# A spectral layer and two MLPs on one core: batch 0's stores moved between batch 1's loads, the inverse 64-point transform on unsplit float32, the front without GpSimd, and the last transform woven into the stages beside it

## Chip, cores and metric

The kernel runs on one core of a Trainium2 chip. The metric is the device time of one execution in microseconds, the median of several runs. Lower is better.

## What is computed

Two batches of 3008 tokens with 256 channels go through a Fourier layer along the tokens, and the 6016 resulting rows through two MLPs with 2048 hidden units. Inputs of the Fourier layer are float32, the MLP weights float64.

```python
X = np.fft.rfft(x, axis=1)                      # x: [2, 3008, 256]
Yr = Xr @ w_r - Xi @ w_i + b_r                  # Xr, Xi: parts of X
Yi = Xr @ w_i + Xi @ w_r + b_i
Y = soft_threshold(Yr, 0.01) + 1j * soft_threshold(Yi, 0.01)
h = np.fft.irfft(Y, n=3008, axis=1).reshape(6016, 256)
h = h @ w_in1;  h = np.maximum(h, 0) + alpha * np.minimum(h, 0)
h = (h @ w_out1) @ w_in2
out = np.where(h >= 1, h, np.where(h <= -1, 0, (h + 1) ** 2 / 4)) @ w_out2
```

## The kernel before

3008 is 47 x 64, so both transforms are made in two radices with matrices as TensorE's operands. The work stands in one written order for each engine; the framework adds the waits.

*Phase 1* (line 254, tiles `ps`, `ae`): 16 groups, 8 for each batch. A group loads 4 rows of `x`, TensorE makes the length-47 transform, ScalarE evicts one half (L256) and VectorE the other (L258) into `ae`, and SP's queue stores it to DRAM (`a_dr`) in two halves of 48 partitions (`store_a(g, 0)` and `store_a(g, 1)`, L223). Batch 0's stores stand after all sixteen loads.

*Phase 2* (L287 to L374): 24 items, 12 for each batch. `f2` (L295) makes the length-64 transform of an item from `a` (read back from `a_dr` by `load_a`, L219) and a third of the matrices in `m_t[i // 4]` (the thirds are called m0 to m2, each good for four items; `n32` holds the inverse ones, n0 to n2). ScalarE copies the result rounded to 12 bits (`fh`, L300) and once more negated (L301); VectorE makes the rest (`fl`, L302) and its negation (L303). `mix` is the complex channel mixing: 24 matmuls, three for each product, with high and low parts. VectorE adds the bias and applies the soft threshold (L320 to L322). `split_y` splits the result into `yh` (ScalarE) and `yl` (GpSimd, L330), and `i1` makes the inverse length-64 transform of it in three matmuls for each of two products. ScalarE evicts into `ve` (L341), two items to a buffer and two buffers in turn (`c2`, `c3`), and SP stores each full buffer to `v_dr`. The matrices for `i1` are split too, into `n_h` (`split_n`). One pass of the loop over j, a step, runs `f2` of item j+2, `mix` of item j and `i1` of item j-2.

*Phase 3*: `p3` reads `v_dr` back as `v` in 16 groups and makes the inverse length-47 transform (L404), transposed, into `y`; each group has two halves c, one evicted by ScalarE (L408) and one by VectorE (L410).

*MLPs* (L413 to L498): 2 layers x 12 chunks of 512 tokens (the sixth of each batch has 448) x 16 blocks f of 128 hidden units. `prep` splits a chunk of `y` into `mxh` and `mxl`, in blocks `c0`, `c1` or `c2`, `c3` in turn (`c0` and `c1` hold the mixing weights `wm` before). `first` makes six matmuls into `psh`; two activations (L431, L432) and a VectorE operation (L433) make the first layer's nonlinearity, whose result is split into `gh` and `gl`; `second`, three blocks behind, adds six matmuls into `pso`.

*Weights*: `conversions` is a generator that turns the float64 weights of block f into a high and a low float32 part (`wt`). A block takes loads into `u` (ScalarE's queue, L127 and L129), three activations (L139, L140, L155), four VectorE operations (L141, L167, L152, L157) and three GpSimd ones (L158, L160, L161). A call of `next(conv)` does half of one block and half of the block beside it; block f of a layer must be ready before `first` of f in chunk 0. Layer 0 has 35 calls.

PSUM has two sets of four buffers, `h` (of `f2`, `first`, one half of `p3`) and `o` (of `mix`, `i1`, `second`, the other half).

Of the kernel before, what the change touches and what calls it, by code (L numbers as in the profile page):

```python
# [75 lines left out]
def spectral_mlp_kernel(ctx: ExitStack, tc: tile.TileContext, x, w_r, w_i, bias, c_f1, c_f2,  # L76
# [152 lines left out]
    for g in range(8):  # L229
        load_x(g)  # L230
    m_t = [block(f"m{k}", [128, 8, 128], F32, f"m{k}") for k in range(3)]
    nc.sync.dma_start(m_t[0][:, 0:4, :].rearrange("p k f -> p (k f)"), c_f2[:, 0:512])
    wm32 = [rot.tile([128, 2, D], F32, tag="tb", name=f"wm32_{k}") for k in range(2)]
    nc.sync.dma_start(wm32[0], w_r.rearrange("(c p) e -> p c e", p=128))
    nc.sync.dma_start(wm32[1], w_i.rearrange("(c p) e -> p c e", p=128))
    nalpha = base.tile([128, NF], F32, name="nalpha")
    nc.sync.dma_start(nalpha, alpha)
    g47 = base.tile([96, 128], F32, name="g47")
    nc.sync.dma_start(g47, c_i2)
    for g in range(8, 16):  # L240
        load_x(g)
    for g in range(16):
# [17 lines left out]
        if g > 7:  # L260
            store_a(g, 1)
        if g == 7:
            load_a(0, A_PARTS[:2])
            nc.sync.dma_start(m_t[0][:, 4:8, :].rearrange("p k f -> p (k f)"), c_f2[:, 512:1024])
            load_a(0, A_PARTS[2:3])
            for k in range(8):
                store_a(k, 1)
            n32 = [block(f"w{k}", [128, 8, 128], F32, f"n32_{k}") for k in range(3)]
            b_t = base.tile([128, 1, D], F32, name="b_t")
            nc.sync.dma_start(b_t[:, 0, :], bias)  # L270
            load_mn(0, n32, c_i1)
            load_mn(1, m_t, c_f2)
            load_a(0, A_PARTS[3:])
            load_mn(1, n32, c_i1)
            load_mn(2, m_t, c_f2)
            load_mn(2, n32, c_i1)
# [4 lines left out]
    n_h = []  # L281

    def split_n(g):
        n_h.append(block(f"m{3 + g}", [128, 2, 4, 128], F32R, f"n{g}"))
        split(n32[g // 2][:, 4 * (g % 2):4 * (g % 2) + 4, :], n_h[g][:, 0], n_h[g][:, 1], A)

# [59 lines left out]
    vs = {}  # L346

    def load_v(g):
        b, j = divmod(g, 8)
        vs[g] = piece([96, 4, D], F32, f"v{b}_{j}")  # L350
        nc.sync.dma_start(vs[g], v_dr[b][:, 4 * j:4 * j + 4, :])

    conv = conversions(0, list(range(NF)), 0)
    n = len(items)
    for j in range(2):
        f2(*items[j])
    for j in range(n):
        if j + 2 < n:
            f2(*items[j + 2])
        if j >= 1:  # L360
            split_y(*items[j - 1])
        mix(*items[j])
        if j + 2 >= n:
            for g in range(2):
                load_v(2 * (j + 2 - n) + g)
        if 5 <= j < 10:
            load_a(1, A_PARTS[j - 5:j - 4])
        if j % 2 == 0 and j < 12:
            split_n(j // 2)
        if j >= 2:  # L370
            i1(*items[j - 2])
        if 4 <= j < 22:
            next(conv, None)
    split_y(*items[n - 1])  # L374

# [19 lines left out]
    y = [block(f"a{b}", [128, 2, S], F32, f"yt{b}") for b in range(B)]  # L395

    def p3(g):
        b, j = divmod(g, 8)
        while len(vs) < min(g + NP, 16):
            load_v(len(vs))  # L400
        ps = [psum.tile([128, 4, 128], F32, tag="ho"[c], name=f"ps3_{b}_{j}_{c}") for c in range(2)]
        for c in range(2):
            for i in range(4):
                T.matmul(ps[c][:, i, :], vs[g][:, i, c * 128:(c + 1) * 128], g47, start=True, stop=True)  # L404
        for c in range(2):
            dst = y[b][:, c, 376 * j:376 * j + 376].rearrange("p (i n) -> p i n", i=4)
            if c == 0:
# [121 lines left out]
```

## Time and profile before

| | |
|---|---|
| runs | 1253.16 us median of 3 (1252.68 to 1253.88) |
| profiled execution | span of 1251.2 us from its first to its last instruction; what lies around the span makes the rest of a run's time |
| TensorE | busy 1214.9 us (97%), weight loads 1030.1 (82%) |
| VectorE | busy 964.8 us (77%) |
| ScalarE | busy 584.6 us (47%) |
| GpSimd | busy 186.2 us (15%) |
| DMA | 59.32 MB, a mean of 47 GB/s |

The shares are means over stages that differ much: in the first hundred microseconds the DMA engines are nearly full, and from about 250 us on they hardly work. PE is TensorE, PEld its weight loads, DVE is VectorE, ACT ScalarE, POOL GpSimd and SP the engine that only issues transfers. ACTq and SPq are the issuing sides of ScalarE and SP.

### The profile page before, as it was taken

To read this page: it belongs to the slowest core of one execution; us is meant where nothing else is said; L and a number is where in the kernel's file an instruction comes from. 1 tells how busy PE (TensorE), PEld (TensorE's weight loads), DVE (VectorE), ACT (ScalarE), POOL (GpSimd) and SP (SyncE) were. 2 spreads that over 40 slices of the span, in tenths; PEclk is the share of its full clock that TensorE was granted. 3 is DMA by queue.
4 is the path that set the end of the run, shared out by engine and by line. 5 is a ranking of instruction groups with operands and counts; after the bars stand their busy time and mean duration, and the time that the engine had idled before them with its cause. 6 is when DMAs were issued, how large, how long until landed. Compare 5 with 4: busy or idle time off the path is not lost.

```text
span 1251.2 us, 15881 instructions
## 1 busy us (share of the span) xinstructions
PE 1214.9 (97%) x5910; PEld 1030.1 (82%) x5910; DVE 964.8 (77%) x1455; ACT 584.6 (47%) x1073; POOL 186.2 (15%) x136
## 2 busy tenths in 40 slices
PE   8898889899999999999999999999999999999998
PEld 6798888688888898888888978888888888888887
DVE  2589977978988899877777798777776777677765
ACT  2355545445455555444444554444444444444443
POOL 0136664401313131300000131000000000000000
PEclk9899999999999999999999999999999999999999
DMA  9983284010000100000000200000000000000000
GB/s 259 304 278 108 87 236 134 1 51 18 30 21 18 34 18 17 1 1 1 1 1 1 65 3 13 5 17 18 1 18 18 15 1 17 17 3 15 17 18 16
DMA packets 37182, 59.32 MB, mean 47 GB/s; under 512 B 3248, under 2 KB 25200, under 8 KB 37104
## 3 DMA queue, kind: packets, MB, share of 16 engines
q1 hardware_dynamic: 23536, 41.37, 10.6%
q10 hardware_dynamic: 13568, 16.93, 4.2%
q8 instruction: 46, 0.75, 0.3%
q14 instruction: 32, 0.26, 0.1%
HBM read 39.55 MB, written 18.74 MB: 47 GB/s over the span
## 4 chain that ended last, share of the span: by engine, by line
PE 83%; DVE 5%; POOL 4%; issue 4%; DMA 2%; ACT 1%; SPq 0%; ACTq 0%; POOLq 0%; DVEq 0%
PE pso L96 13%; PE pso L95 13%; PE pso L97 13%; PE psh L96 13%; PE psh L95 13%; PE psh L97 13%; PE ps L404 2%; POOL yl L330 2%; DMA x<-in_x 1%; DVE gl L92 1%; DVE ta L433 1%; PE ps L254 1%; DVE gh L91 1%; POOL cm L160 1%; PE psf L295 1%
## 5 line engine op out<-in xcount | busy, mean ns | idle before, releaser
L96 PE MATMUL pso<-gl,w 128*128 128x512 f32 (+1 forms) x768 | 298.8, 389 | 6.2 <-DVE gl L92 6.2
L95 PE MATMUL pso<-gh,w 128*128 128x512 f32 (+1 forms) x768 | 297.1, 387 | 3.9 <-DVE gh L91 3.9
L96 PE MATMUL psh<-mxl,w 128*128 128x512 f32 (+1 forms) x768 | 297.2, 387 | 0.0
L95 PE MATMUL psh<-mxh,w 128*128 128x512 f32 (+1 forms) x768 | 296.9, 387 | 0.0
L97 PE MATMUL pso<-gh,w 128*128 128x512 f32 (+1 forms) x768 | 296.3, 386 | 0.0
L97 PE MATMUL psh<-mxh,w 128*128 128x512 f32 (+1 forms) x768 | 295.9, 385 | 0.0
L92 DVE TENSOR_TENSOR gl<-ta,gh 128x512 fp32r<-128x512 f32 (+1 forms) x384 | 280.1, 729 | 7.2 <-ACT gh L89 0.6
L437 ACT ACTIVATE ta<-psh 128x512 f32<-128x512 f32 (+1 forms) x192 | 113.1, 589 | 281.3 <-PE psh L97 247.1
L438 DVE SCALAR_TENSOR_TENSOR tb<-ta 128x512 f32<-128x512 f32 (+1 forms) x192 | 131.2, 683 | 137.5 <-ACT ta L437 136.5
L431 ACT ACTIVATE ta<-psh 128x512 f32<-128x512 f32 (+1 forms) x192 | 113.1, 589 | 250.8 <-PE psh L97 211.8
L433 DVE SCALAR_TENSOR_TENSOR ta<-ta,nalpha,tb 128x512 f32<-128x512 f32 (+1 forms) x192 | 168.9, 880 | 64.3 <-ACT tb L432 63.7
L96 PEld LDWEIGHTS pso<-gl,w 128*128 128x128 f32 x768 | 144.5, 188 | 36.9 <-DVE gl L92 10.5
L95 PEld LDWEIGHTS pso<-gh,w 128*128 128x128 f32 x768 | 144.3, 188 | 33.4 <-DVE gh L91 5.3
L95 PEld LDWEIGHTS psh<-mxh,w 128*128 128x128 f32 x768 | 144.5, 188 | 28.4
L97 PEld LDWEIGHTS psh<-mxh,w 128*128 128x128 f32 x768 | 144.3, 188 | 27.7
L97 PEld LDWEIGHTS pso<-gh,w 128*128 128x128 f32 x768 | 144.5, 188 | 27.3
L96 PEld LDWEIGHTS psh<-mxl,w 128*128 128x128 f32 x768 | 144.4, 188 | 27.0
L440 DVE TENSOR_TENSOR ta<-psh,tb 128x512 f32<-128x512 f32 (+1 forms) x192 | 129.2, 673 | 0.0
L89 ACT ACTIVATE gh<-ta 128x512 fp32r<-128x512 f32 (+1 forms) x192 | 118.3, 616 | 2.0 <-DVE ta L440 2.0
L158 POOL TENSOR_TENSOR cp<-cp,u 128x512 f32<-128x512 f32 x32 | 44.7, 1397 | 462.4 <-DVE cp L157 454.0
L432 ACT ACTIVATE tb<-psh 128x512 f32<-128x512 f32 (+1 forms) x192 | 112.4, 585 | 0.0
L91 DVE CAST gh<-ta 128x512 fp32r<-128x512 f32 (+1 forms) x192 | 91.1, 474 | 19.5
(62 smaller groups left out, 1067.3 us busy)
## 6 DMA issues: line engine op xcount, KB each, us to landing
u<-in_w_in ACTq DMA_DIRECT2D x32, 256.0 KB, 2.8
u<-in_w_out ACTq DMA_DIRECT2D x32, 256.0 KB, 3.0
v_dr<-ve SPq DMA_DIRECT2D x12, 512.0 KB, 3.3
v<-v_dr SPq DMA_DIRECT2D x16, 384.0 KB, 7.1
x<-in_x SPq DMA_DIRECT2D x15, 384.0 KB, 8.8
out<-yt SPq DMA_DIRECT2D x20, 256.0 KB, 2.2
a<-a_dr SPq DMA_DIRECT2D x6, 768.0 KB, 7.9
a_dr<-ae SPq DMA_DIRECT2D x20, 192.0 KB, 7.9
```

The costliest lines, as they stand in the source:

```text
L89: A.activation(hi, src, AF.Copy)
L91: V.tensor_copy(hi, src)
L92: V.tensor_tensor(lo, src, hi.bitcast(F32), op=ALU.subtract)
L95: T.matmul(ps, wl, xh, start=start, stop=False)
L96: T.matmul(ps, wh, xl, start=False, stop=False)
L97: T.matmul(ps, wh, xh, start=False, stop=stop)
L431: A.activation(ta, ps, AF.Relu, scale=-1.0)
L432: A.activation(tb, ps, AF.Relu)
L433: V.scalar_tensor_tensor(ta, ta, nalpha[:, f:f + 1], tb, op0=ALU.mult, op1=ALU.add)
L437: A.activation(ta, ps, AF.Relu, bias=0.5, scale=0.5)
L438: V.scalar_tensor_tensor(tb, ta, 1.0, ta, op0=ALU.min, op1=ALU.mult)
L440: V.tensor_tensor(ta, ps, tb, op=ALU.max)
```

## The change

- Phase 1: `store_a(g, 0)` of batch 0 stands right after its group, between the loads of batch 1; the second halves follow all loads. Batch 1's groups store their first halves together and then their second halves. `load_a(1)` follows these in one piece, with nalpha and g47 ahead of it.
- `i1` takes float32 operands as they are, one matmul for each product in place of three; `split_y`, `split_n` and their tiles go. The matrices are called `n_t`.
- The negation L303 is ScalarE's.
- Layer 0's conversions run wholly on VectorE and ScalarE; layer 1's on GpSimd as before, started at chunk 2 instead of chunk 1.
- `p3` of batch 0 stands in steps 16 to 23 of phase 2, one group a step; that of batch 1 in the first MLP, one half with each block from block 4 of chunk 0 to block 3 of chunk 1, evicted by ScalarE. `v` has buffers of its own.
- In chunk 0 the split of the activation is one block late and its high part is ScalarE's.
- `prep(0, 0)` stands in step 22.

```diff
-    def convert_w(l, f, part, clamp=None):
+    def convert_w(l, f, part, clamp, low_engine):
+        E = low_engine
...
-            G.tensor_tensor(p, p, low, op=ALU.mult)
+            E.tensor_tensor(p, p, low, op=ALU.mult)
...
-            G.tensor_tensor(m, m, wt[l, f][:, 0, :].bitcast(F32), op=ALU.subtract)
-            G.tensor_tensor(wt[l, f][:, 1, :], m, p, op=ALU.add)
+            E.tensor_tensor(m, m, wt[l, f][:, 0, :].bitcast(F32), op=ALU.subtract)
+            E.tensor_tensor(wt[l, f][:, 1, :], m, p, op=ALU.add)
...
+    for g in range(8):
+        f1(g)
         store_a(g, 0)
...
+        load_x(8 + g)
+        if g == 3:
+            nc.sync.dma_start(m_t[0][:, 0:4, :].rearrange("p k f -> p (k f)"), c_f2[:, 0:512])
...
+    load_a(0, A_PARTS[:3])
+    nc.sync.dma_start(m_t[0][:, 4:8, :].rearrange("p k f -> p (k f)"), c_f2[:, 512:1024])
+    nc.sync.dma_start(b_t[:, 0, :], bias)
+    load_mn(0, n_t, c_i1)
+    for g in range(8):
+        store_a(g, 1)
+    load_mn(1, m_t, c_f2)
+    load_a(0, A_PARTS[3:])
+    for g in range(8, 16):
+        f1(g)
+        store_a(g, 0)
+    load_mn(1, n_t, c_i1)
+    for g in range(8, 16):
+        store_a(g, 1)
+    load_mn(2, m_t, c_f2)
+    load_mn(2, n_t, c_i1)
+    nc.sync.dma_start(nalpha, alpha)
+    nc.sync.dma_start(g47, c_i2)
+    load_a(1, A_PARTS)
...
-        V.tensor_scalar(xl[:, :, 0:64], xl[:, :, 128:192].bitcast(F32), -1.0, None, op0=ALU.mult)
+        A.mul(xl[:, :, 0:64], xl[:, :, 128:192].bitcast(F32), -1.0)
...
-            q, r = divmod(2 * i + k, 4)
-            mm3(ps[:, k, :], n_h[q][:, 0, r, :], n_h[q][:, 1, r, :], yh[:, k, :], yl[:, k, :], True, True)
+            T.matmul(ps[:, k, :], n_t[i // 4][:, (2 * i + k) % 8, :], y32[:, k, :], start=True, stop=True)
...
+    def late_split(step):
+        return step[0] == 1 or step[:2] == (0, 0)
+
     def split_late(step):
-        if step is not None and step[0] == 1:
+        if step is not None and late_split(step):
...
+    conv = conversions(0, list(range(NF)), V, V)
...
+        if j == 13:
+            for g in range(3):
+                load_v(g)
+        if j >= P3_AT:
+            g = j - P3_AT
+            p3(g, 0, A)
+            p3(g, 1, V)
+            if g + 3 < 8:
+                load_v(g + 3)
+        if j == n - 2:
+            prep(0, 0)
+        for _ in range((j >= 3 and j % 3 != 0) if j < P3_AT else 1 + j % 2):
             next(conv, None)
...
+    i1(*items[n - 2])
+    first(0, 0, 0, None)
+    i1(*items[n - 1])
+    for g in range(8, 16):
+        load_v(g)
+    first(0, 0, 1, (0, 0, 0))
...
-            if (l, c, f) == (0, 1, 0):
+            if (l, c, f) == (0, 2, 0):
...
+            if 4 <= i < 20:
+                p3(8 + (i - 4) // 2, i % 2, A)
```

The order on the engines at three places. SP, at the end of `x`'s loads, before the change: here `x` ends and the first halves of batch 0 (`a_dr_0_68`) follow, and then the first read (`a`).

```order
L209 DMA x_5_121<-in_x 96x1024
L209 DMA x_6_123<-in_x 96x1024
L209 DMA x_7_125<-in_x 96x1024
L223 DMA a_dr_0_68<-ae_127 48x4x256
L223 DMA a_dr_0_68<-ae_137 48x4x256
```

The same place after the change.

```order
L224 DMA a_dr_0_68<-ae_173 48x4x256
L210 DMA x_5_183<-in_x 96x1024
L224 DMA a_dr_0_68<-ae_185 48x4x256
L210 DMA x_6_195<-in_x 96x1024
L224 DMA a_dr_0_68<-ae_197 48x4x256
L210 DMA x_7_207<-in_x 96x1024
L220 DMA a_209<-a_dr_0_68 128x512
```

The stores now alternate with the loads, and the first read stands right behind the last load of `x`.

SP again, where phase 2 begins to store (`v_dr`), before the change: `a_652` is batch 1's `a`.

```order
L223 DMA a_dr_0_70<-ae_late 48x4x256
L223 DMA a_dr_1_71<-ae_late 48x4x256
L344 DMA v_dr_72<-ve_0_488 128x4x256
L219 DMA a_652<-a_dr_0_70 128x512
L344 DMA v_dr_72<-ve_2_599 128x4x256
L219 DMA a_652<-a_dr_0_70 128x1024
L219 DMA a_652<-a_dr_0_70 128x1536
L344 DMA v_dr_72<-ve_4_724 128x4x256
```

After it, where `a_315` is batch 1's `a`.

```order
L227 DMA m_101<-in_c_f 128x1024
L227 DMA n_104<-in_c_i 128x1024
L282 DMA nalpha<-in_alpha 128x16
L283 DMA g_108<-in_c_i 96x128
L220 DMA a_315<-a_dr_0_70 128x512
L220 DMA a_315<-a_dr_0_70 128x1024
L220 DMA a_315<-a_dr_0_70 128x1536
L220 DMA a_315<-a_dr_1_71 128x1536 x2
L339 DMA v_dr_72<-ve_0_479 128x4x256
L339 DMA v_dr_72<-ve_2_573 128x4x256
```

Batch 1's reads stood between the first `v_dr` stores; now all of them, and the last matrices, stand ahead of the first. On ScalarE the same time of the program, step 4 and on, reads after the change:

```order
L336 ACTIVATE ve_2_573<-psi_2_570 128x512
L127 DMA u_0_575<-in_w_in 128x2x256
L129 DMA u_0_575<-in_w_out 128x512
L127 DMA u_1_578<-in_w_in 128x2x256
L129 DMA u_1_578<-in_w_out 128x512
L303 ACTIVATE fh_7_586<-psf_7_581 128x4x128
L304 ACTIVATE fh_7_586<-psf_7_581 128x4x64
L306 ACTIVATE fl_7_587<-fl_7_587 128x4x64
L336 ACTIVATE ve_2_573<-psi_3_623 128x512
L140 ACTIVATE cm_0_628<-u_0_575 128x512
L141 ACTIVATE u_0_575<-u_0_575 128x512
L303 ACTIVATE fh_8_638<-psf_8_633 128x4x128
```

The four loads of `u` stand where they stood before, between the eviction of `i1` 2 and those of `f2` 7; new is L306, the negation.

VectorE from the end of step 22 to the first block of the MLP, after the change (`psm_11` is `mix` of item 23, L378 a `p3` eviction, L405 the operation that was L433):

```order
L92 TENSOR_TENSOR mxl_0_1640<-yt_1202,mxh_0_1639 128x1024
L158 TENSOR_SCALAR cp_7_1580<-cm_7_1579 128x512
L159 TENSOR_TENSOR cp_7_1580<-cp_7_1580,u_7_1436 128x512
L142 TENSOR_SCALAR cp_8_1648<-u_8_1513 128x512
L324 TENSOR_TENSOR t_11_1678<-psm_11_1652,b_t 128x512
L325 TENSOR_SCALAR clip_11_1677<-t_11_1678 128x512
L326 TENSOR_TENSOR y_1_11_1679<-t_11_1678,clip_11_1677 128x512
L378 COPY yt_1202<-ps_0_7_1_1694 128x376
L161 TENSOR_TENSOR cm_7_1579<-cm_7_1579,w_7_1643 128x512
L162 TENSOR_TENSOR w_7_1643<-cm_7_1579,cp_7_1580 128x512
L168 TENSOR_SCALAR cm_8_1647<-cm_8_1647 128x512
L153 SCALAR_TENSOR_TENSOR cm_8_1647<-cm_8_1647,cp_8_1648 128x512
```

`mxl` stood in the middle of phase 3 before; now it stands ahead of the last thresholds, with conversions on both sides of these. L159, L161 and L162 were GpSimd's.

## Rows read from the trace of the kernel before

**Rows 1.** Stages: stretch, length, busy us and instructions by engine, PEclk, DMA share, GB/s.

```profile
98.80:168.29 69.49, 57.66 (x448) 54.72 (x447) 67.97 (x89) 33.88 (x67) 45.70 (x32) 0.98 0.35 113
...
198.86:252.66 53.80, 45.96 (x193) 35.22 (x192) 47.91 (x67) 25.35 (x47) 22.02 (x15) 0.97 0.06 21
252.66:1251.20 998.54, 992.25 (x4435) 831.83 (x4433) 770.43 (x1182) 469.69 (x854) 82.94 (x60) 1.00 0.05 15
...
296.32:339.97 43.65, 43.65 (x193) 36.04 (x192) 39.08 (x56) 22.65 (x41) 10.94 (x8) 1.00 0.08 25
```

**Rows 2.** TensorE in order of time: start, us, what, [idle before <-releaser].

```profile
8.24 10.60 PE L254 MATMUL ps<-x,c 96*96 96x256 f32 x48 [0.28 <-DMA x<-in_x]
...
52.67 2.04 PE L295 MATMUL psf<-m,a 128*128 128x128 f32 x8 [2.96 <-DMA m<-in_c_f]
...
63.16 1.05 PE L295 MATMUL psf<-m,a 128*128 128x128 f32 x8
63.97 0.36 PE L315 MATMUL psm<-wm,fl 128*128 128x256 f32 x1
...
66.89 0.28 PE L95 MATMUL psi<-yh,n 128*128 128x256 f32 x1
...
67.60 1.06 PE L295 MATMUL psf<-m,a 128*128 128x128 f32 x8
...
171.02 3.74 PE L404 MATMUL ps<-g,v 96*128 96x128 f32 x32
174.51 0.36 PE L95 MATMUL psi<-yh,n 128*128 128x256 f32 x1
```

**Rows 3.** VectorE in order of time, in phase 2.

```profile
95.10 0.68 DVE L302 TENSOR_TENSOR fl<-psf,fh 128x512 fp32r<-128x512 f32 x1
...
96.03 0.68 DVE L320 TENSOR_TENSOR y<-psm,b_t 128x512 f32<-128x512 f32 x1
96.75 0.43 DVE L321 TENSOR_SCALAR clip<-y 128x512 f32<-128x512 f32 x1
97.21 0.69 DVE L322 TENSOR_TENSOR y<-y,clip 128x512 f32<-128x512 f32 x1
97.82 0.42 DVE L157 TENSOR_SCALAR cp<-cm 128x512 uint32<-128x512 uint32 x1
98.16 0.42 DVE L141 TENSOR_SCALAR cp<-u 128x512 uint32<-128x512 uint32 x1
...
112.99 1.66 DVE L322 TENSOR_TENSOR y<-y,clip 128x512 f32<-128x512 f32 x1
```

**Rows 4.** GpSimd's groups from 38 to 253 us: busy, mean ns, idle before.

```profile
L158 POOL TENSOR_TENSOR cp<-cp,u 128x512 f32<-128x512 f32 x16 | 22.7, 1417 | 57.8 <-DVE cp L157 49.4 <-ACT ta L431 8.4
```

**Rows 5.** Waits from 38 to 200 us: in total, times, longest.

```profile
PE psi L96 <- POOL yl L330: 9.5, 8, 2.0
```

**Rows 6.** DMA engines from 35 to 38 us, 40 slices: GB/s.

```profile
GB/s 0 0 0 0 0 0 0 0 0 0 0 0 0 0 0 0 0 0 0 0 27 82 191 164 218 82 82 164 218 300 410 410 328 300 355 328 383 219 328 273
```

**Rows 7.** ScalarE in order of time: the smaller copy of `f2`.

```profile
70.52 0.38 ACT L301 ACTIVATE fh<-psf 128x256 fp32r<-128x256 f32 x1
```

**Rows 8.** SP's waits over the whole span.

```profile
SPq L223 <- DMA u<-in_w_in: 6.3, 2, 5.5
```

**Rows 9.** Two stretches with full DMA engines; columns as in the first group.

```profile
10.00:30.00 20.00, 18.17 (x77) 13.15 (x76) 6.67 (x10) 5.33 (x9) 0.00 (x0) 0.91 1.04 268
36.50:62.00 25.50, 20.73 (x147) 20.16 (x148) 15.51 (x27) 9.22 (x20) 3.27 (x3) 0.87 1.00 342
```

**Rows 10.** Transfers issued from 79 to 81 us: KB each, us to landing.

```profile
a<-a_dr SPq DMA_DIRECT2D x1, 768.0 KB, 8.9
...
u<-in_w_in ACTq DMA_DIRECT2D x1, 256.0 KB, 9.1
```

**Rows 11.** The same for 67 to 69 us.

```profile
u<-in_w_in ACTq DMA_DIRECT2D x2, 256.0 KB, 3.5
```

**Rows 12.** VectorE in chunk 0, with GpSimd idle.

```profile
242.88 0.75 DVE L433 SCALAR_TENSOR_TENSOR ta<-ta,nalpha,tb 128x512 f32<-128x512 f32 x1
```

More of the change, by code (lines that the diff above doesn't have):

```diff
@@ L167, in clamp_w, with conversions @@
         engine.tensor_scalar(m, m, W_MAX, W_MIN, op0=ALU.min, op1=ALU.max)
-    def conversions(l, fs, on_pool):
+    def conversions(l, fs, clamp, low_engine):
         n = len(fs)
@@ L228, in spectral_mlp_kernel, with f1 @@
     a_sb, aes = [None] * B, {}
[L229 to L242, printed above, removed]
+    def f1(g):
         b, j = divmod(g, 8)
         if g < 10:
-            ae = block(f"w{8 + g}" if g < 5 else f"m{g - 2}", [96, 4, D], F32, f"ae{g}")
+            ae = block(f"w{8 + g}" if g < 5 else f"m{1 + g}" if g < 8 else f"w{g - 8}", [96, 4, D], F32, f"ae{g}")
         else:
             if g == 10:
-                late = block("a1", [96, 6, 4, D], F32, "ae_late")
-            ae = late[:, g - 10]
+                late.append(block("a1", [96, 6, 4, D], F32, "ae_late"))
+            ae = late[0][:, g - 10]
         aes[g] = ae
@@ L258, in spectral_mlp_kernel @@
                 V.tensor_copy(ae[:, 2:4, :], ps)
-        store_a(g, 0)
[L260 to L276, printed above, removed]
+    late = []
+    for g in range(8):
+        load_x(g)
+    m_t = [block(f"m{k}", [128, 8, 128], F32, f"m{k}") for k in range(3)]
+    n_t = [block(f"m{3 + k}", [128, 8, 128], F32, f"n{k}") for k in range(3)]
+    wm32 = [rot.tile([128, 2, D], F32, tag="tb", name=f"wm32_{k}") for k in range(2)]
+    nalpha = base.tile([128, NF], F32, name="nalpha")
+    g47 = base.tile([96, 128], F32, name="g47")
+    b_t = base.tile([128, 1, D], F32, name="b_t")
+    for g in range(8):
+        f1(g)
+        store_a(g, 0)
+        load_x(8 + g)
+        if g == 3:
+            nc.sync.dma_start(m_t[0][:, 0:4, :].rearrange("p k f -> p (k f)"), c_f2[:, 0:512])
+            nc.sync.dma_start(wm32[0], w_r.rearrange("(c p) e -> p c e", p=128))
+            nc.sync.dma_start(wm32[1], w_i.rearrange("(c p) e -> p c e", p=128))
+    load_a(0, A_PARTS[:3])
+    nc.sync.dma_start(m_t[0][:, 4:8, :].rearrange("p k f -> p (k f)"), c_f2[:, 512:1024])
+    nc.sync.dma_start(b_t[:, 0, :], bias)
+    load_mn(0, n_t, c_i1)
+    for g in range(8):
+        store_a(g, 1)
[12 more added lines that the diff above has]
+    load_a(1, A_PARTS)
     wm = [block(f"c{k}", [128, 2, 2, D], F32R, f"wm{k}") for k in range(2)]
@@ L280, in spectral_mlp_kernel @@
     V.tensor_scalar(nalpha, nalpha, -1.0, None, op0=ALU.mult)
[L281 to L285, printed above, removed]
     items = [(b, i) for b in range(B) for i in range(NK // 2)]
-    xt, yt, y_32, ve = {}, {}, {}, {}
+    xt, y_32, ve = {}, {}, {}
     def f2(b, i):
@@ L344, in i1 @@
             nc.sync.dma_start(dst[:, 2 * i - 2:2 * i + 2, :], ve[b])
[L346 to L374, printed above, removed]
     chunks = []
@@ L393, in prep, with load_v, p3 @@
         xc[l, c] = xh, xl
-    y = [block(f"a{b}", [128, 2, S], F32, f"yt{b}") for b in range(B)]
-    def p3(g):
+    vs, y = {}, [None] * B
+    def load_v(g):
         b, j = divmod(g, 8)
[L399 to L407, printed above, removed]
-                A.activation(dst, ps[c][:, :, 0:94], AF.Copy)
-            else:
-                V.tensor_copy(dst, ps[c][:, :, 0:94])
+        vs[g] = block(f"m{6 + g % 3}" if b == 0 else f"m{j}", [96, 4, D], F32, f"v{b}_{j}")
+        nc.sync.dma_start(vs[g], v_dr[b][:, 4 * j:4 * j + 4, :])
+    def p3(g, c, engine):
+        b, j = divmod(g, 8)
+        if y[b] is None:
+            y[b] = block(f"a{b}", [128, 2, S], F32, f"yt{b}")
+        ps = psum.tile([128, 4, 128], F32, tag="h", name=f"ps3_{b}_{j}_{c}")
+        for i in range(4):
+            T.matmul(ps[:, i, :], vs[g][:, i, c * 128:(c + 1) * 128], g47, start=True, stop=True)
+        dst = y[b][:, c, 376 * j:376 * j + 376].rearrange("p (i n) -> p i n", i=4)
+        if engine is A:
+            A.activation(dst, ps[:, :, 0:94], AF.Copy)
+        else:
+            V.tensor_copy(dst, ps[:, :, 0:94])
+    def late_split(step):
+        return step[0] == 1 or step[:2] == (0, 0)
     def split_late(step):
-        if step is not None and step[0] == 1:
+        if step is not None and late_split(step):
             gh, gl, ta = gt[step]
@@ L432, in first @@
             A.activation(tb, ps, AF.Relu)
+            split_late(before)
             V.scalar_tensor_tensor(ta, ta, nalpha[:, f:f + 1], tb, op0=ALU.mult, op1=ALU.add)
-            split(ta, gh, gl, V)
+            if not late_split((l, c, f)):
+                split(ta, gh, gl, V)
         else:
@@ L461, in second @@
                     nc.sync.dma_start(out[:, e, b * S + c0:b * S + c0 + n], dst)
-    for g in range(16):
-        p3(g)
-        if g in (0, 2):
-            i1(*items[g // 2 - 2])
-        if g % 2 == 0:
-            next(conv, None)
-        if g == 10:
-            prep(0, 0)
-        if g >= 14:
-            first(0, 0, g - 14, None)
+    conv = conversions(0, list(range(NF)), V, V)
+    n = len(items)
+    P3_AT = 16
+    for j in range(2):
+        f2(*items[j])
+    for j in range(n):
+        if j + 2 < n:
+            f2(*items[j + 2])
+        mix(*items[j])
+        if j >= 2:
+            i1(*items[j - 2])
+        if j == 13:
[10 more added lines that the diff above has]
+        for _ in range((j >= 3 and j % 3 != 0) if j < P3_AT else 1 + j % 2):
+            next(conv, None)
+    i1(*items[n - 2])
[4 more added lines that the diff above has]
+    first(0, 0, 1, (0, 0, 0))
     DEPTH = 3
@@ L478, in spectral_mlp_kernel @@
             l, c, f = seq[i]
-            if (l, c, f) == (0, 1, 0):
+            if (l, c, f) == (0, 2, 0):
                 for _ in conv:
                     pass
-                conv = conversions(1, list(range(12)), NF)
+                conv = conversions(1, list(range(12)), G, G)
             if (l, c, f) == (0, NC - 1, 4):
@@ L485, in spectral_mlp_kernel @@
                     pass
-                conv = conversions(1, list(range(12, 16)), 0)
+                conv = conversions(1, list(range(12, 16)), V, G)
             if i >= 2:
                 first(l, c, f, seq[i - 1])
-            if (l, c) == (0, 0) and f < 15 or f % 2 == 0 and (c == 0 or f % 4 == 0 or (l, c) == (0, NC - 1)):
+            if 4 <= i < 20:
+                p3(8 + (i - 4) // 2, i % 2, A)
+            if ((l, c) == (0, 0) and f < 15 or (l, c) in ((0, NC - 1), (1, 0)) and f % 2 == 0
+                    or l == 0 and c >= 2 and f % 4 == 0):
                 next(conv, None)
```

26 lines of the change are left out of this document (10 added, 16 removed).

## Prediction

> **What bounds the kernel now.** I read the stages first [rows 1]: from 252.66 us to the end TensorE is busy 992 of 998.5 us, so this part moves only if something is added to it. What can be won lies before. There, in the 69.5 us from 98.80 on, VectorE is busy 67.97 and TensorE 57.66: VectorE is the bound. The stage from 198.86 on, the first chunk of the first MLP, takes 53.8 us with TensorE busy 46.
>
> Then TensorE's own pace, from rows without a wait [rows 2]. Step j of phase 2 does `f2` of item j+2, `mix` of item j and `i1` of item j-2; a step repeats in 4.44 us (63.16 to 67.60): `f2` 0.81, `mix` 2.92, `i1` 0.71. Unsplit float32 matmuls of 256 columns are two records each, 0.215 us apart (48 records in 10.6 us). A pair of `p3` halves, 16 records, takes 1.745 us (32 from 171.02 to 174.51). A chunk of the MLP without a wait takes 43.65 us [rows 1] for 16 `first` and 16 `second`: 1.364 each.
>
> From 38.31, the first `f2`, to 252.66 TensorE's work by these paces is 24 x 4.44 + 16 x 1.745 + (16 + 13) x 1.364 = 174 us of 214: it waits 40. The question is how much of that remains.
>
> Who makes it wait: with GpSimd at work the same VectorE instruction takes 1.66 us instead of 0.69 (L322 at 112.99 and at 97.21), while L302 and L320, which read PSUM, take 0.68 [rows 3]. GpSimd's own operations take 1.4 us [rows 4], and TensorE waits 9.5 us for `yl` [rows 5]. One more wait, 2.96 us for the second third of the matrices (m1), stands before `f2` of item 4, at 52.67 [rows 2].
>
> **The change part by part.** The sum follows TensorE through the profiled execution, whose span of 1251.2 us is 1.96 us under the median of the runs, 1253.16.
>
> *Start.* The stores between loads move the same bytes ahead of m1 as before. What goes is an idle stretch: from 35 to 36.5 us the DMA engines moved nothing, since the last stores had to land before the first read back [rows 6]; now x's last loads lie there. I take 2 us off 52.67, so `f2` 4 stands at 50.5. Bounds: 49.4, by when the work before it ends, and 53.7, a microsecond late. The bias also comes before the stores, but TensorE's next wait was for m1 anyway.
>
> *Steps.* Unsplit, `i1` is four records of 0.215, so 0.86 instead of 0.71: a step is 4.60 us, 3.7 us more over 24. For it go 24 conversions on ScalarE and 24 GpSimd subtractions, and six splits of the matrices; they hid behind other work except where VectorE was the bound. The negation L303 leaves VectorE for ScalarE, where I price it as L301, which has its size, 0.38 [rows 7]; it stands two steps ahead of its `mix`. Without GpSimd, VectorE's step is 0.72 + 0.72 + 0.46 + 0.61 = 2.5 us from start to start [rows 3]. A converted block now adds GpSimd's three operations to its four: 0.46 + 0.61 + 0.34 + 0.72 + 0.61 + 0.46 + 0.61 = 3.8 us, 1.9 a call. No row has those three on VectorE: below stands L322 with 0.69, above GpSimd's 1.4 [rows 4]; I take 0.69, the same engine with two operands of that size in SBUF (0.61 to the next start, 0.72 where the next needs the result). Steps 3 to 15 carry two calls in three: 3.8 of 4.6 us, hidden. Steps 16 to 23 carry 1.5 calls and a `p3` eviction, some 0.5: 5.9 of the 6.34 us that TensorE needs with a `p3` pair: hidden, with 0.4 to spare.
> 14 x 4.60 (steps 2 to 15) + 6 x 6.34 (16 to 21) + 5.53 (22, no `f2`) + 2.92 (`mix` 23) = 110.9: `mix` 23 ends at 161.4.
>
> *The queues.* `load_a(1)` now stands whole ahead of the first `v_dr` store, behind all batch-1 stores, m2, n2 and two small loads (nalpha, g47); ScalarE's first weight loads `u` come after these. A DMA issue can wait for a landing on the other queue: SP's stores waited 6.3 us for `u` [rows 8]. So I expect ScalarE, in step 4, not to issue `u` until g47 and the start of `a` have landed. Behind it stand the evictions of `f2` 7, then the conversion that needs `u`, then the evictions of `f2` 8; `mix` 8 waits for the last. From 36.5 on 10.9 MB, by the shapes, precede the end of g47. At that stretch's 342 GB/s [rows 9] they land at 68.4; ScalarE arrives at 64.7. `u`, issued beside reads of `a`, took 9.1 us [rows 10]: 78; then 3.3 us of work on ScalarE and VectorE to `mix` 8: 81.3, against 78.9 by pace. That is 2.4 us; at the 268 GB/s of the x loads [rows 9] it is 10.7; if `u` lands in 3.5 us, as from 67.8 on [rows 11], nothing. I take 4, nearer the first: 165.4.
>
> The Trainium skill (DMA: Bandwidth & Descriptors, "Queues, rings and completion order") says that each DMA engine takes turns between the queues, packet by packet; by that, ScalarE's 256 KB should not wait for SP's 768 KB. The trace speaks against it: both landed some 9 us after issue [rows 10]. By the rule the wait is nothing and the sum 4 us less.
>
> *First chunk.* TensorE's work from the end of `mix` 23 to chunk 1: three `i1`, a `p3` pair, 16 `first`, 13 `second`, 12 `p3` halves: 2.6 + 1.7 + 39.6 + 10.5 = 54.4. VectorE has more. `prep(0, 0)` overwrites `wm`'s blocks, so its split waits for `mix` 23 on ScalarE and VectorE, and step 22's call, item 23's thresholds, an eviction and two calls queue behind: 1.1 + 1.2 + 1.4 + 1.8 + 0.5 + 3.8 = 10 us. Then each MLP step costs it 0.60 (`gl`) + 0.80 (L433, 0.75 and a gap [rows 12]) + 1.9 = 3.3 us. Block 15 is ready after two calls (3.8), twelve such steps, a `prep` of 1.2 and 5 us of splits: 59.6 us; `first` 15 and what follows it add 3.6. ScalarE and VectorE hand over to each other twice a step, for which I add 2.3: 65.5, of which TensorE waits 11. Bounds: 57 (the lag nearly hidden) and 72. Chunk 1 starts at 230.9, against 252.66.
>
> *Rest.* 998.5 as before, and the four `p3` halves that fall into chunk 1, 3.5 (no conversions run there): 1232.9. With the 1.96: **1235 us**.
>
> **The rivals.**
> *The weight loads do not wait behind SP's*: by the 3.5 us row [rows 11] `mix` 8 is on time, 1231. This is what the skill's rule gives.
> *Neither lag shows*: `mix` 8 on time and chunk 0 in 57 us, 161.4 + 57 + 1002 + 2 = 1222. For it: VectorE's load is near TensorE's pace, not far above. Against: block 15 has one step of slack.
> *The queue waits longer*, at 268 GB/s: 10.7 instead of 4, 1242. For it: the x loads moved no faster.
> *VectorE becomes the bound, and the kernel slower.* Forty of the 48 new operations fall into steps 16 to 23 and chunk 0. If each costs e more than priced, the end moves by 40 e less the 3.5 us of slack. At GpSimd's 1.4 us [rows 4] e is 0.79: 28 us, 1263. It decides from e = 0.54, an operation of 1.15 us. For it: L158 reads every second word, and no two-input VectorE row does. Against: L141 reads so in 0.42 us [rows 3].
> *No change*: the front's gain eaten exactly; only a point between these.
>
> **How the numbers follow.** Chances: forecast 0.57; loads not behind SP's 0.18; neither lag 0.08; longer queue 0.11; VectorE the bound 0.04; no change 0.02. Faster by over 0.2% (2.5 us, about what a measurement of this kernel can tell from none): 0.94; within: 0.02; slower: 0.04. The forecast's own terms (start 49.4 to 53.7, chunk 0 from 60 to 72) span 1228 to 1245. The range for 8 in 10, 1224 to 1248, takes in the longer queue with a late start, and reaches towards the case without lags; it leaves out that case's lower half and the last two.
>
> **What would show it.** Right: `psi` in four records of 0.215; L322's successor at 0.69 throughout; TensorE without gaps from step 9 to 22, at 4.6 and 6.3 us a step; one wait of some microseconds before `mix` 8, with ScalarE standing in a DMA issue or before the conversion; VectorE near full in chunk 0, `first` 14 and 15 waiting for their weights; chunk 1 at about 231, then 998 and 3.5. Wrong: L158's operation far over 0.69 on VectorE; gaps at `p3` for `v`; ScalarE, with some 3 us of work a step in chunk 0, the one waited for; stalls in later chunks that were not there.

## The result

The changed kernel takes 1261.2 us (median of 4 runs, 1260.42 to 1265.17); the kernel before, measured beside it, 1252.92. The ratio is 1.007, with a 95% interval from 1.0053 to 1.0087: slower by 8 us, where 18 us faster was forecast. The profiled execution took 1261.51 us, its span 1259.7.

**One hole.** TensorE in order of time after the change (columns as in [rows 2]):

```profile
34.39 1.06 PE L298 MATMUL psf<-m,a 128*128 128x128 f32 x8
35.70 1.13 PE L298 MATMUL psf<-m,a 128*128 128x128 f32 x8 [0.25 <-DMA a<-a_dr]
38.81 1.13 PE L298 MATMUL psf<-m,a 128*128 128x128 f32 x8 [1.98 <-DMA m<-in_c_f]
71.09 0.58 PE L318 MATMUL psm<-wm,fl 128*128 128x256 f32 x1 [31.15 <-DVE fl L305]
```

After the first three `f2`, TensorE stands for 31.15 us before `mix` of item 0, for VectorE's `fl`. What `fl` waits for is not `fh` or a matrix: VectorE in order of time,

```profile
35.20 1.28 DVE L92 TENSOR_TENSOR wm<-wm,wm 128x512 fp32r<-128x512 f32 x2
70.27 0.17 DVE L288 TENSOR_SCALAR nalpha<-nalpha 128x16 f32<-128x16 f32 x1 [33.79 <-DMA nalpha<-in_alpha]
70.35 0.69 DVE L305 TENSOR_TENSOR fl<-psf,fh 128x512 fp32r<-128x512 f32 x1
```

and the issues on SP's queue:

```profile
59.58 3.75 SPq L224 DMA_DIRECT2D a_dr<-ae_late  x5
63.37 0.55 SPq L227 DMA_DIRECT2D m<-in_c_f  x1
63.97 0.72 SPq L227 DMA_DIRECT2D n<-in_c_i  x1
64.73 0.43 SPq L282 DMA_DIRECT2D nalpha<-in_alpha  x1
```

An instruction of 0.17 us, the negation of nalpha, stands in VectorE's queue between the split of `wm` and the first `fl`. Its 8 KB are first used in the first MLP, but the negation waits where it stands, and everything behind it with it. Before, nalpha was loaded among the first things; the change puts its load behind all batch-1 stores, m2 and n2, where it is issued at 64.73.

**The rest.** Stages after the change (columns as in [rows 1]):

```profile
40.70:71.10 30.40, 0.01 (x1) 0.01 (x1) 0.77 (x2) 0.03 (x1) 0.00 (x0) 0.50 0.95 298
...
98.80:168.29 69.49, 69.49 (x564) 68.01 (x563) 54.03 (x95) 36.61 (x77) 0.00 (x0) 1.00 0.42 129
188.60:257.60 69.00, 59.61 (x301) 49.61 (x300) 56.10 (x96) 47.06 (x90) 0.00 (x0) 0.95 0.38 107
257.60:1259.70 1002.10, 996.18 (x4467) 835.39 (x4465) 770.15 (x1182) 471.82 (x859) 83.05 (x60) 1.00 0.04 15
```

In the hole the DMA engines are full (0.95) and the compute engines idle. From 98.80 to 168.29, where TensorE was busy 57.66 us before [rows 1], it now has no gap, and VectorE has room (54.03, was 67.97). The first chunk, from the end of `mix` 23 to chunk 1, takes 69.0 us, and what follows it 1002.1.

### The profile page after: what moved, and what is told of

The parts are those of the page before. It is cut to its first block, busy times and chain, and to the rows that moved or that the text cites. A ratio compares the mean times of both kernels' runs of the same rounds, so it can differ in the third digit from the quotient of the medians.

```text
span 1259.7 us, 15641 instructions
## 1 busy us (share of the span) xinstructions
PE 1208.5 (96%) x5862; PEld 1026.6 (81%) x5862; DVE 926.3 (74%) x1449; ACT 588.7 (47%) x1091; POOL 83.3 (7%) x64
## 3 DMA queue, kind: packets, MB, share of 16 engines
q1 hardware_dynamic: 23536, 41.37, 10.5%
## 4 chain that ended last, share of the span: by engine, by line
PE 90%; DVE 3%; DMA 3%; SPq 2%; ACT 1%; issue 1%; ACTq 0%; DVEq 0%
PE pso L96 13%; PE pso L95 13%; PE psh L95 13%; PE psh L96 13%; PE pso L97 13%; PE psh L97 13%; PE ps L373 2%; PE psm L318 2%; PE psm L320 2%; PE psm L319 2%; PE ps L243 2%; PE psf L298 1%; PE psi L333 1%; SPq L224 1%; DMA a_dr<-ae 1%; DVE gl L92 1%
## 5 line engine op out<-in xcount | busy, mean ns | idle before, releaser
L92 DVE TENSOR_TENSOR gl<-ta,gh 128x512 fp32r<-128x512 f32 (+1 forms) x384 | 277.1, 722 | 18.1 <-ACT gh L89 12.0
L405 DVE SCALAR_TENSOR_TENSOR ta<-ta,nalpha,tb 128x512 f32<-128x512 f32 (+1 forms) x192 | 166.4, 867 | 64.0 <-ACT tb L403 63.4
L89 ACT ACTIVATE gh<-ta 128x512 fp32r<-128x512 f32 (+1 forms) x208 | 128.4, 617 | 2.0 <-DVE ta L413 2.0
L91 DVE CAST gh<-ta 128x512 fp32r<-128x512 f32 (+1 forms) x176 | 79.6, 452 | 18.1
L318 PE MATMUL psm<-wm,fl 128*128 128x256 f32 x192 | 56.3, 293 | 31.2 <-DVE fl L305 31.2
```

What stands on the lines that cost most here:

```text
L318: T.matmul(o, xl[:, j, off:off + 128], wm[r][:, 0, c, :], start=c == r == 0, stop=False)
L405: V.scalar_tensor_tensor(ta, ta, nalpha[:, f:f + 1], tb, op0=ALU.mult, op1=ALU.add)
```

## The experiments

The theory: VectorE's wait for nalpha is the 31 us, and without it the sum of the prediction holds. Rivals: the wait is for other work of the new front (the `fl` negation on ScalarE, the loads as a whole), or the time is lost in the conversions that VectorE took over. Twelve kernels were run; all times are medians, with the ratio to the kernel before, measured beside each (that kernel's median was 1252.5 to 1254.3). The two columns of starts come from the profiled execution.

| kernel | us | ratio, 95% interval | first MLP step | chunk 1 |
|---|---|---|---|---|
| changed | 1261.2 | 1.0070, 1.0053 to 1.0087 | 192.01 | 257.60 |
| e1: nalpha early | 1239.1 | 0.9896, 0.9872 to 0.9920 | 168.94 | 234.75 |
| e2: negation late | 1238.8 | 0.9888, 0.9869 to 0.9907 | 167.25 | 234.15 |
| e3: before, nalpha late | 1268.0 | 1.0117, 1.0099 to 1.0135 | 213.09 | 266.78 |
| e4: e1, low words on GpSimd | 1243.1 | 0.9917, 0.9895 to 0.9939 | 169.34 | 238.38 |
| e5: e1, m2 early | 1240.8 | 0.9905, 0.9871 to 0.9940 | 169.89 | 236.36 |
| e6: e5, five calls earlier | 1235.8 | 0.9863, 0.9834 to 0.9892 | 173.29 | 232.05 |
| e8: before, unsplit `i1` | 1237.7 | 0.9873, 0.9844 to 0.9903 | 183.75 | 237.52 |
| e9: e5, x's loads first | 1246.3 | 0.9947, 0.9928 to 0.9965 | 175.58 | 242.40 |
| e10: e5, `a` spread | 1230.7 | 0.9821, 0.9802 to 0.9840 | 160.89 | 226.48 |
| e11: e10, five calls earlier | 1225.9 | 0.9786, 0.9767 to 0.9805 | 166.69 | 224.28 |
| e13: e10, low words on GpSimd | 1234.4 | 0.9851, 0.9834 to 0.9867 | 160.36 | 231.31 |
| e14: e10, three calls earlier | 1221.3 | 0.9750, 0.9736 to 0.9765 | 158.66 | 217.36 |

**e1, e2 and e3: is it nalpha, and is it the load or the place of the instruction?**

```
e1:  load_x, at g == 3, behind wm32[1]
+            nc.sync.dma_start(nalpha, alpha)
     ... behind load_mn(2, n_t, c_i1)
-    nc.sync.dma_start(nalpha, alpha)
e2:  behind the split of wm
-    V.tensor_scalar(nalpha, nalpha, -1.0, None, op0=ALU.mult)
     ... ahead of first(0, 0, 0, None)
+    V.tensor_scalar(nalpha, nalpha, -1.0, None, op0=ALU.mult)
e3:  the kernel before, nalpha's load moved to behind
             load_mn(2, n32, c_i1)
+        nc.sync.dma_start(nalpha, alpha)
```

> Only the place of the load of nalpha differs from the changed kernel: it is issued behind wm32, as early as in the kernel before, instead of behind batch 1's stores. Theory (VectorE's negation of nalpha, which stands ahead of every fl on that engine, waits for the load and holds phase 2): mix of item 0 starts at about 40 instead of 71.09 us, 31 us are given back, and two smaller waits come into sight that the long one covered: f2 of item 8 for m2 (lands 68.7, wanted at about 65: 4 us) and mix 8 for the first weight blocks (0 to 5 us). Total 1232 to 1239, against 1261 for the changed kernel. Rival 1 (the wait is for f2's own evictions, with the negation of fl now on ScalarE, or for the stretch of loads as a whole): mix 0 stays at about 71 and the time at 1259 to 1262. Rival 2 (the slow-down sits in VectorE's conversions in chunk 0): the same, 1259 to 1262.

> The load of nalpha stays behind batch 1's stores as in the changed kernel; only VectorE's instruction that negates it is emitted later, just ahead of the first step of the first MLP, where it is first used. Theory (it is the place of the waiting instruction in VectorE's queue that costs, not the late load): the same as with the early load, within 1.5 us of it, 1232 to 1239. Rival (the late load delays through SP's queue or the DMA engines): no gain, 1259 to 1262.

> The kernel before, with the load of nalpha moved behind its last load of phase 2's matrices (n32 2, which lands at about 62 us) and nothing else. Theory: VectorE's fl of item 0 waits for it, mix 0 starts at about 63 instead of 42.9 us; of these 20 us some 3 are paid back by the wait for m1 that is then covered: slower by 15 to 20 us, 1268 to 1273. Rival (a load of 8 KB is of no account): within 1 us of 1253.

e1 gives back 22 us of the 31, e2 the same within 0.3 us: the late load in itself costs nothing that shows; the waiting instruction's place in VectorE's order costs everything. The kernel before, with only that load moved, loses 13.6 us (15 to 20 expected). In its trace, first VectorE and then TensorE:

```profile
59.10 0.17 DVE L280 TENSOR_SCALAR nalpha<-nalpha 128x16 f32<-128x16 f32 x1 [24.02 <-DMA nalpha<-in_alpha]
```

```profile
59.92 0.58 PE L315 MATMUL psm<-wm,fl 128*128 128x256 f32 x1 [16.55 <-DVE fl L302]
```

Both rivals expected no gain from e1 and fall. But 9 of the 31 us come back as another wait. TensorE in e1:

```profile
63.38 1.02 PE L333 MATMUL psi<-y,n 128*128 128x256 f32 x4
72.65 2.07 PE L298 MATMUL psf<-m,a 128*128 128x128 f32 x8 [8.25 <-DMA m<-in_c_f]
```

`f2` of item 8 waits for m2. Some 4 us of this were expected, from m2's place behind batch 1's stores. The rest comes from SP's own waits in e1, from 55 to 70 us (in total, times, longest), and m2's issue behind them:

```profile
SPq L224 <- DMA n<-in_c_i: 2.6, 1, 2.6
SPq L224 <- DMA u<-in_w_out: 2.3, 1, 2.3
SPq L224 <- DMA u<-in_w_in: 2.0, 1, 2.0
...
SPq L227 <- DMA u<-in_w_out: 0.6, 1, 0.6
```

```profile
67.90 0.35 SPq L227 DMA_DIRECT2D m<-in_c_f  x1
```

SP's stores and then m2 itself are not issued until ScalarE's `u` have landed; in the changed kernel, where ScalarE itself stood still and issued no `u` then, m2 was issued at 63.37. `u`, issued at 60 to 62.5, landed in 4.0 to 5.4 us (medians of two).

**e5, e10: what stands behind that wait?** e5 loads m2 right behind m1; e10 also spreads the loads of `a`.

```
e5:  load_mn(1, m_t, c_f2)
+    load_mn(2, m_t, c_f2)
     ... (and no longer behind batch 1's stores)
e10: - load_a(1, A_PARTS)
     ... in step j of phase 2, behind mix
+        if 4 <= j < 9:
+            load_a(1, A_PARTS[j - 4:j - 3])
```

> The early load of nalpha, and besides it the last third of phase 2's matrices (m2) is loaded right behind the second (m1) instead of behind batch 1's stores. With nalpha early, f2 of item 8 still waited 8.25 us for m2, whose issue in SP's queue had waited for the landing of ScalarE's weight loads u. Theory (the queue term of the forecast is this wait, with m2 as what is late, and nothing stands behind it): f2 8 on time at about 64.4, 8.3 us and the 1.7 us of half clock behind the wait are given back, total 1228 to 1231. Rival of the prediction (ScalarE's u is late in any case and mix 8 waits for it, so the wait only moves): 1234 to 1239.

> As the kernel with nalpha and m2 early, and the five loads of a for batch 1 issued one in each of the steps 4 to 8 of phase 2, as in the kernel before, instead of whole ahead of the first v_dr store. With m2 early, ScalarE's eviction ve of item 4 stood 15.55 us for the landing of the first v_dr store at 84.9 us, whose block it overwrites, and TensorE 8.1 us behind it. Theory (the loads of a ahead of that store in SP's queue make it late; the sum's queue term is this wait): the store lands at about 74, TensorE's gap of 8.1 us and some 2 us of half clock go, 1228 to 1232. Rival (it is ScalarE's u and the batch-1 stores ahead of both that are late, and the gap only shrinks to 4 us or goes over to f2 for a): 1234 to 1241.

e5 gains nothing: `f2` 8 is on time, and TensorE stands 8.1 us two steps later, in `i1` of item 6, whose PSUM buffer waits to be evicted. TensorE and then ScalarE in e5:

```profile
85.68 2.07 PE L333 MATMUL psi<-y,n 128*128 128x256 f32 x4 [8.09 <-ACT ve L336]
```

```profile
69.06 0.42 ACT L306 ACTIVATE fl<-fl 128x256 fp32r<-128x256 f32 x1 [0.76 <-DVE fl L305]
85.03 0.60 ACT L336 ACTIVATE ve<-psi 128x512 f32<-128x512 f32 x1 [15.55 <-DMA v_dr<-ve]
```

The eviction of item 4 overwrites the block that the first `v_dr` store reads, and that store stands in SP's queue behind the whole of `load_a(1)`. So the rival of e5 held in kind: the wait moved, though not to `u`, and 1240.8 lies just above the rival's range. With the loads of `a` spread, TensorE in e10 has no such wait (ScalarE still stands 6.1 us for that landing, instead of 15.55): steps repeat in 4.48 us from 62.65 to 107.45, and the time is 1230.7, inside the theory's range.

**e6, e11 and e14: the conversions' lag in chunk 0.**

```
e6, e11: for _ in range((j >= 3) if j < P3_AT else 1 + j % 2):
e14:     for _ in range((j >= 4 and (j % 3 != 0 or j >= 9)) if j < P3_AT else 1 + j % 2):
```

> As the kernel with nalpha and m2 early, and a conversion call in each of the steps 3 to 15 of phase 2 instead of in two of three (five calls earlier, so ten instead of fifteen are left for chunk 0). Theory (VectorE's conversions are late in chunk 0 by about 11 us of TensorE's time, of which 5 to 6 are the waits before first 14, 15 and the start of chunk 1): 4 to 8 us faster than with m2 early alone, 1221 to 1226, VectorE busy 4.4 of 4.6 us in steps 3 to 15 and no gaps there. Rival (VectorE is then the bound in phase 2, and what is won in chunk 0 is lost there): within 2 us of it, 1227 to 1232.

> All the repairs together: nalpha and m2 early, the loads of a for batch 1 spread over steps 4 to 8, and a conversion call in each of the steps 3 to 15. Theory (with the call in each step alone TensorE still lost 10.5 us to the same wait for the v_dr store): 1222 to 1226. Rival (VectorE, at 4.4 of 4.6 us a step in phase 2, cannot keep pace without the pause that the wait gave it): 1228 to 1236.

> As the kernel with nalpha and m2 early and a spread, with three more conversion calls, in steps 9, 12 and 15. The kernel with a call in each of the steps 3 to 15 gained 8 us in chunk 0 but lost 6 in phase 2, where a third block's weight loads had come ahead of the batch-1 stores and the first v_dr store landed at 79.6. Theory (only the early calls cost, through the queues): phase 2 as with a spread (the first MLP step starts at about 161), chunk 0 in 59 to 62 instead of 65.6 us: 1224 to 1228. Rival (VectorE, near full in these steps, is late itself): chunk 0's gain is lost in phase 2 again, 1228 to 1231.

e6 is 5 us faster than e5, within the 4 to 8 expected; its total misses the range, because e5 had not gained and TensorE in e6 still stands 10.5 us for the same eviction. From the first MLP step to chunk 1 e10 takes 65.6 us, e11 57.6 and e14 58.7. e11 loses 5.8 us of that ahead of it: its calls begin a step earlier, a third block's `u` (issued at 67.7) comes ahead of the first `v_dr` store, which is issued at 73.55 and lands at 79.56, and ScalarE in e11 stands for it again:

```profile
79.67 0.60 ACT L335 ACTIVATE ve<-psi 128x512 f32<-128x512 f32 x1 [8.10 <-DMA v_dr<-ve]
```

e14 adds calls only from step 9 on and keeps both, so it is the early calls that cost. It is the best of all, 2.5% under the kernel before, and almost 3 us under the range expected: 2.4 us of its lead over e10 were there at `f2` of item 4 already (45.79 against 48.19), which no edit explains. TensorE's waits in e14 from 30 to 280 us:

```profile
PE psf L297 <- DMA m<-in_c_f: 2.1, 2, 1.4
PE ps L372 <- DMA v<-v_dr: 1.9, 1, 1.9
PE psi L332 <- DVE y L325: 1.3, 1, 1.3
PE psf L297 <- DMA a<-a_dr: 1.3, 1, 1.3
PE pso L95 <- ACT gh L89: 0.9, 1, 0.9
```

**e4, e9, e8 and e13: what the parts are worth.** e4 and e13 put the low words of layer 0 back on GpSimd, in e1 and in e10; e9 issues all loads of x ahead of the stores, in e5; e8 is the kernel before with nothing but the unsplit transform.

```
e4, e13: conv = conversions(0, list(range(NF)), V, G)
e9:  all load_x(8) to load_x(15) ahead of the first f1, as in the kernel before
e8:  i1 as in the change, on n32 and y32; split_n and split_y go; y32 takes the four buffers of yh
+            T.matmul(ps[:, k, :], n32[i // 4][:, (2 * i + k) % 8, :], y32[:, k, :], start=True, stop=True)
```

> The early load of nalpha, and the three operations of a layer-0 conversion that make the low word back on GpSimd (p times low, m minus the high word, the sum), as in the kernel before; the clamp stays on VectorE. Theory of the prediction (VectorE's operations with two inputs in SBUF take 1.66 us instead of 0.69 while GpSimd works, and a handover is added): slower than the early load alone by 5 to 15 us, 1240 to 1252. Rival (VectorE, which gets 1.9 us a block fewer, is the bound in chunk 0, and the relief is worth more than the slowed operations): faster by 3 to 8 us, 1226 to 1233.

> As the kernel with nalpha and m2 early, but x's loads of batch 1 are all issued ahead of batch 0's stores, as in the kernel before (with the first half of m0, wm32 and nalpha between the two batches). Theory (storing batch 0 between the loads is worth the stretch in which no DMA moved anything, about 2 us, and up to 4 us at the first f2, and nothing behind it absorbs it): slower than with m2 early alone by 2 to 5 us. Rival (the work up to f2 0 is bound by the bytes moved alone): within 1 us.

> The kernel before, and of the change only the inverse 64-point transform on unsplit float32: no split of the matrices n and of y, so 24 conversions on ScalarE and 24 subtractions on GpSimd go, and i1 is two float32 matmuls. Theory (the split's work and TensorE's waits for yl, 9.5 us in the kernel before, cost more than the 3.7 us that float32 adds on TensorE): faster by 4 to 10 us, 1243 to 1249. Rival (VectorE stays the bound in phase 2 with GpSimd's conversions beside it, and the wait only goes over to another of its results): within 2 us of before; and if only TensorE counts, slower by 3.7 us, 1257.

> As the kernel with nalpha and m2 early and a spread, but the three operations that make the low word of a layer-0 conversion go back to GpSimd. With nalpha alone early, this cost 4.0 us (1243.1 against 1239.1), while another wait still hid part of phase 2. Theory (a front without GpSimd is worth something, but little, since VectorE has room in phase 2): slower than with a spread by 2 to 6 us, 1233 to 1237. Rival of the prediction (GpSimd at work slows VectorE's two-input operations to 1.66 us and VectorE becomes the bound of phase 2 again): slower by 10 us or more, from 1241 on. Other rival (the relief of VectorE in chunk 0 outweighs both): faster by 2 us or more, below 1229.

e9 is 5.4 us slower than e5 (2 to 5 expected) and its `f2` of item 4 stands at 53.09 instead of 46.73. e8 surprised: alone, the unsplit transform gains 15.6 us (4 to 10 expected), about 70% of what e10 gains (21.8). VectorE's groups in e8 from 100 to 160 us (busy, mean ns):

```profile
L323 DVE TENSOR_TENSOR y<-t,clip 128x512 f32<-128x512 f32 x13 | 14.9, 1143 | 0.5
...
L152 DVE SCALAR_TENSOR_TENSOR cm<-cm,cp 128x512 uint32<-128x512 uint32 x6 | 4.2, 692 | 0.2
...
L167 DVE TENSOR_SCALAR cm<-cm 128x512 f32<-128x512 f32 x6 | 2.5, 415 | 0.0
```

the last two of these lines in the kernel before, in the same stretch:

```profile
L167 DVE TENSOR_SCALAR cm<-cm 128x512 f32<-128x512 f32 x6 | 9.1, 1514 | 0.0
L152 DVE SCALAR_TENSOR_TENSOR cm<-cm,cp 128x512 uint32<-128x512 uint32 x6 | 9.0, 1497 | 0.2
```

and e8's stage from 100 to 146 us:

```profile
100.00:146.00 46.00, 46.00 (x370) 44.94 (x369) 44.72 (x74) 23.40 (x47) 20.09 (x15) 1.00 0.36 122
```

GpSimd still converts there, and VectorE's threshold instruction with two inputs in SBUF (L323) still takes 1.14 us on average, but TensorE has no gap: without `yl` and the splits, VectorE, busy 44.72 of 46, just keeps the step of 4.48 to 4.58 us. VectorE's own conversions are faster too: L167 takes 0.42 us instead of 1.51 and L152 0.69 instead of 1.50. In the kernel before, L152 mostly ran beside `yl` on GpSimd, and L167 mostly beside a conversion that stood behind a `yl`; in e8, neither runs beside a GpSimd instruction in this stretch. The unsplit transform is thus already a part of a front without GpSimd. Taking the rest of GpSimd out is then worth little: e4 is 4.0 us over e1 (5 to 15 expected) and e13 3.7 over e10 (2 to 6 expected; their intervals overlap, but both traces place it in chunk 0, from the first MLP step to chunk 1: 69.0 against 65.8 and 70.9 against 65.6). TensorE's waits in e13:

```profile
PE psh L95 <- ACT tb L402: 3.3, 2, 3.1
PE psh L95 <- POOL w L162: 3.2, 2, 2.5
```

## Why the prediction was wrong

The working was made against the span; it forecast 1232.9 and 1259.7 was measured, 26.8 more. By its steps: `f2` of item 4 at 79.41 instead of 50.5 (+28.9); from there to the end of `mix` 23 109.2 instead of 114.9 (-5.7: a shorter step, and none of the 4 us of the queues, which the hole covered); the first chunk 69.0 instead of 65.5 (+3.5); the rest 1002.1 instead of 1002.0.

**The step that failed** is *The queues* with *Start*: "behind all batch-1 stores, m2 and n2 and two small loads (nalpha, g47)". The moved load was counted as bytes that others wait behind. Who waits for it was not asked, and the sum has nothing for that wait; it took 31.15 us of TensorE's time. Its consumer stands on VectorE ahead of all of phase 2, and an in-order engine passes the wait on to everything behind. e1, e2 and e3 show it from three sides. No rival held it either: "VectorE becomes the bound, and the kernel slower" had the engine, with another mechanism.

**The other steps**, by the profile of the changed kernel and e1:

- *Start*, apart from nalpha: better than its lower bound of 49.4. In e1 `f2` of item 4 starts at 46.11, with no wait for m1, which landed at 44.97; e9 measures the reordering at 5.4 us, where 2 were taken. A stretch without transfers around the first read back remains: in the changed kernel the DMA engines moved nothing for 0.6 us from 31.5 on.
- *Steps*: right. `i1` is four records, 0.86 us to the next start; a step is 4.48 instead of 4.60, because `mix` takes 2.81 and not the 2.92 of before, and 6.37 with a `p3` pair (6.34). ScalarE's L306 takes 0.42 (0.38 taken). VectorE's new operations take what was priced, in the changed kernel from 100 to 160 us:

```profile
L159 DVE TENSOR_TENSOR cp<-cp,u 128x512 f32<-128x512 f32 x4 | 2.8, 692 | 0.1
L162 DVE TENSOR_TENSOR w<-cm,cp 128x512 fp32r<-128x512 f32 x4 | 2.8, 692 | 0.1
L161 DVE TENSOR_TENSOR cm<-cm,w 128x512 f32<-128x512 f32 x4 | 2.7, 684 | 0.0
```

- *The queues*, the wait before `mix` 8: that issues on one queue wait for landings of the other is right, but the direction is not. ScalarE issues `u` on time in e1, SP waits for it, and what comes late is m2 (8.25 us) and, behind that, the block of `ve` (8.1 in e5). Priced at 4 with a bound of 10.7; in e1 the wait, with the half clock behind it, makes the two steps there 10.1 us longer than 4.48 each. The place, `load_a(1)` whole ahead of the first `v_dr` store, was named; that the block under `ve` comes free only when this store has landed was not.
- In e1 `u` landed in 4.0 to 5.4 us beside SP's traffic, not in the 9.1 of [rows 10]. The rule of the Trainium skill (DMA: Bandwidth & Descriptors, "Queues, rings and completion order"), that each DMA engine takes turns between the queues, fits that. But e1 does not decide for it, because SP's own issues were held back during a part of that time. The waits that cost time there were for issues held back on SP.
- *First chunk*: right in kind, 3.5 us short. Its waits in the changed kernel, from 200 to 258 us:

```profile
202.16 0.50 PE L95 MATMUL pso<-gh,w 128*128 128x512 f32 x1 [2.84 <-ACT gh L89]
...
208.24 2.07 PE L373 MATMUL ps<-g,v 96*128 96x128 f32 x8 [2.59 <-DMA v<-v_dr]
247.74 0.47 PE L95 MATMUL psh<-mxh,w 128*128 128x512 f32 x1 [1.16 <-ACT yt L376]
253.86 0.47 PE L95 MATMUL psh<-mxh,w 128*128 128x512 f32 x1 [2.23 <-DVE w L162]
```

  The last steps' waits are the lag, as forecast; the wait for `v`, which the text had only as a sign of being wrong, is new at this place. TensorE ran at half clock from 207.9 to 214.7 us, around that wait.
- *Rest*: right to 0.1 us.

With nalpha early, e1 has the first MLP step at 168.94; the sum puts it at 165.4 + 0.86 + 1.75 + 0.86 (two `i1` and a `p3` pair) = 168.9. That agreement is partly luck: the start was 4.4 us earlier and the steps nearly 2 us cheaper, which hid a queue some 6 us dearer than taken. e1's 1239.1 against 1235 is the first chunk.

What stays open: how much weaving the last transform alone brings was not tried apart. The parts that were tried (15.6 of e8, 5.4 of e9, 3.7 of e13) already sum to more than the 21.8 us of e10; whether they add up like this, and whether weaving then gains anything, no run shows. Why the first chunk's steps 3 and 4 take 4.4 to 8.5 us each in every version with the last transform woven in, where most later steps take 3.63, was not followed up.

## What to carry to other kernels

When a load moves back in a queue, find the instruction that consumes it and look at what stands behind that instruction on its engine, however small both are; emit a preparation next to its first use, not with the set-up. A store frees its source block only when it has landed, so a load put ahead of it in the queue can stop an eviction much later. And when a long wait goes, expect shorter ones that it covered: here removing 31 us gave 22, and two more repairs in the same queue were needed for the rest.

## What the runs showed of the hardware

- VectorE beside GpSimd, in e8:

```profile
110.05 0.69 DVE L323 TENSOR_TENSOR y<-t,clip 128x512 f32<-128x512 f32 x1
...
114.18 1.67 DVE L323 TENSOR_TENSOR y<-t,clip 128x512 f32<-128x512 f32 x1
```

```profile
111.21 1.35 POOL L158 TENSOR_TENSOR cp<-cp,u 128x512 f32<-128x512 f32 x1 [4.80 <-DVE cp L157]
112.52 1.34 POOL L160 TENSOR_TENSOR cm<-cm,w 128x512 f32<-128x512 f32 x1
113.94 1.37 POOL L161 TENSOR_TENSOR w<-cm,cp 128x512 fp32r<-128x512 f32 x1
```

  The average of 1.14 us has no instruction near it: from 100 to 160 us L323 took 0.69 in all seven cases without a GpSimd instruction beside it and 1.67 in all six with one. A one-input instruction of 512 elements (L324 in e13, the clip) took 0.43 us without and 0.78 to 1.34 with one. In e8 this costs TensorE nothing from 100 to 146 us, where VectorE's step just fits.
- Issues on SP waited for landings of ScalarE's transfers: 4.9 us in total in e1 (2.3 + 2.0 + 0.6).
- Through the idle 31 us TensorE's granted clock was 0.50, that is 1.2 of its 2.4 GHz, and so it was for the first matmuls after them: 24 matmuls of 256 columns in `mix` of item 0 took 5.41 us to the next start of `mix`, `f2` included, against 3.72 for the next.
